# First loads, first sums and the last addition of a two-branch linear-attention kernel in another order

## The chip, the cores and the metric

The kernel runs on one core of a Trainium2 chip. The metric is the device time of one execution in microseconds (us), lower is better. The engines of the core are TensorE (PE; its weight loads are listed as PEld), VectorE (DVE), ScalarE (ACT), GpSimd (POOL) and SyncE (SP). SP computes nothing here: it issues most of the transfers (DMA). ACT issues some as well.

## The reference

```python
def _A_ref(x, wqkv, wo):                       # _B_ref is the same
    B, S, D = x.shape                          # 1, 2048, 640
    H = 32; Dh = D // H
    qkv = (x @ wqkv).reshape(B, S, 3, H, Dh).transpose(2, 0, 3, 1, 4)
    q, k, v = qkv[0], qkv[1], qkv[2]
    phi = lambda t: jnp.where(t > 0, t + 1, jnp.exp(t)) + 1e-6
    pq, pk = phi(q), phi(k)
    kv = jnp.einsum("bhsd,bhse->bhde", pk, v)
    z = jnp.einsum("bhsd->bhd", pk)
    num = jnp.einsum("bhqd,bhde->bhqe", pq, kv)
    den = jnp.einsum("bhqd,bhd->bhq", pq, z)[..., None] + 1e-6
    return (num / den).transpose(0, 2, 1, 3).reshape(B, S, D) @ wo

x = A_x
g = sigmoid((x * gate_w).sum(-1, keepdims=True))
return g * _A_ref(x, A_wqkv, A_wo) + (1 - g) * _B_ref(x, B_wqkv, B_wo)
```

All inputs and the output are bf16. There are 16 row chunks of 128 rows (P = 128), and 640 columns are 5 column chunks (DT = 5) or two halves of HF = 320.

## The kernel before

The kernel works in stages that follow each other on PE. For branch A it makes the k projection with `phi` for all row chunks, mixed with the first half of the q projection; then the rest of q; then the products of x with `phi(k)` (tiles g and gs), from which kv follows; then the same for branch B; then the output, in eight pairs of row chunks, from seven products each (p1 to p7, a Strassen scheme).

*The first stage.* x has to be turned, since PE contracts over partitions: the tile xT holds x transposed, in 5 column chunks. Rows 0 to 255 (chunks 0 and 1) are loaded plain into xn (`load_x`, L116) and turned on PE with an identity matrix (`x_transpose`, L200) into a PSUM tile xt, from which DVE copies to xT (L203). All other rows are turned by the transfer itself (`x_turned`, L119). The k weights wkA are loaded by column chunks (`load_wk`, L122), the q weights wqA in three pieces. A column beside wkA holds `gate_w`, so that the gate's logits come out of the second half of the k sums as a 321st column: gate_w is loaded as five rows (L125), turned on PE (L162), copied by DVE (L164) and written into wkA by POOL (L166).

Before the first data PE runs seven matmuls on constants (L160, tile warm). Then `k_first` makes the k sums of chunks 0 to 3. `k_mm` (L221) is one matmul: a row chunk i, a column chunk c, and a half hf of the columns, into a PSUM tile kA of two banks. Chunks 0 and 1 go together through c = 0 to 2, then each through c = 3 and 4; then chunks 2 and 3 one after the other. `k_done` hands a sum to `phi`: an exponential on ACT (L208), a minimum and an addition on DVE (L213), the maximum with 1 + src on DVE (L217); ACT also copies the logit (L227).

PSUM is handed out in four slots (`ps`), each a tile of two banks; the next user of a slot waits for the last reader of the one before. The first q block (L278), which follows `k_first`, takes slot 2; the next takes slot 3, then come q_single (L288) in slot 0 and chunk 4 in slot 1.

*Order.* The order on each engine in `k_first` and in the output stage is the order in the code (`tc.manual_schedule()`). Eight semaphores serve the transfers in turn, so from the ninth transfer on an issue can wait for the landing of the one eight before it, and holds up its queue meanwhile.

*The end.* A pair's methods are: p7 makes a product on top of the one of p6 in bank x and DVE adds it into one row half (`out_add`, L575); p2 with c11, p4 and p3 make the others. `u25` adds the copy u6 of p6's product and p15 into v, on DVE. Only p3 reads v. The last pair stores its halves separately (L589), two on ACT's queue and two on SP's, and p3 in two parts of 160 columns.

Of the kernel before, what the change touches and what calls it, by code (L numbers as in the profile page):

```python
# [8 lines left out]
P = 128  # L9
FP32 = mybir.dt.float32  # L10
BF16 = mybir.dt.bfloat16
# [3 lines left out]
S, D, H = 2048, 640, 32  # L15
Dh = D // H
DT = D // P
ST = S // P
NB = 4
CB = 4  # L20
HB = 512
HF = D // 2
# [9 lines left out]
def kernel(  # L32
# [11 lines left out]
    nc = tc.nc  # L44
# [13 lines left out]
    def ps_raw(name, slot=None):  # L58

        if slot is None:  # L60
            slot = turn[0]
            turn[0] = (slot + 1) % 4
        return psum.tile([P, 4 * HB], BF16, tag=f"ps{slot}", name=name)

    def ps(name, slot=None):

        return ps_raw(name, slot).bitcast(FP32).rearrange("p (b n) -> p b n", b=2)
# [43 lines left out]
    wk = [None, None]  # L111
# [3 lines left out]
    def load_x(eng, i):  # L115
        eng.dma_start(out=xn[:, i, :], in_=x2[i * P:(i + 1) * P, :])  # L116

    def x_turned(lo, hi):
        nc.sync.dma_start_transpose(out=xT[:, :, lo:hi], in_=x2[lo:hi, :])  # L119

    def load_wk(eng, lo, hi):
        eng.dma_start(out=wk[0][:, lo:hi, 0:D], in_=wq_dram[0][:, lo:hi, D:2 * D])  # L122

    grow = R[0][0:DT, 0:P]
    nc.scalar.dma_start(out=grow, in_=gate_w.rearrange("(c p) -> c p", p=P))  # L125
    load_x(nc.sync, 0)
    load_x(nc.scalar, 1)
    for c, eng in enumerate((nc.sync, nc.scalar, nc.sync, nc.scalar, nc.sync)):
        load_wk(eng, c, c + 1)
    x_turned(2 * P, HB)  # L130
    wq[0] = wpool.tile([P, DT, D], BF16, tag="wq", name="wqA")
    for lo, hi in ((0, 2), (2, 4), (4, DT)):
        nc.sync.dma_start(out=wq[0][:, lo:hi, :], in_=wq_dram[0][:, lo:hi, 0:D])
    for n in range(1, NB):
        x_turned(n * HB, (n + 1) * HB)


    make_identity(nc, ident[:])
# [17 lines left out]
    raw = ps_raw("warm", 3)  # L156
    warm = raw.bitcast(FP32).rearrange("p (b n) -> p b n", b=2)
    one_l, one_r = [nc.const_aps.tensor(1.0, [P, n], BF16) for n in (P, HB)]
    for k in range(7):
        nc.tensor.matmul(warm[:, 0, :], lhsT=one_l, rhs=one_r, start=True, stop=True)  # L160
    gcol = raw[:, 2 * HB:2 * HB + DT]
    nc.tensor.transpose(out=gcol, in_=grow, identity=ident[0:DT, 0:DT])  # L162
    gsb = work.tile([P, DT], BF16, tag="rT", name="gsb")
    nc.vector.tensor_copy(out=gsb[:], in_=gcol)  # L164
    for c in range(DT):
        nc.gpsimd.tensor_copy(out=wk[0][:, c, D:D + 1], in_=gsb[:, c:c + 1])  # L166

    def by_group(dst, lhsT, src, h):

# [28 lines left out]
    def x_transpose(i, pt, cuts=(0, DT)):  # L198
        for c in range(DT):
            nc.tensor.transpose(out=pt[:, c * P:(c + 1) * P], in_=xn[:, i, c * P:(c + 1) * P], identity=ident[:])  # L200
        src = pt[:, 0:D].rearrange("p (c n) -> p c n", c=DT)
        for lo, hi in zip(cuts, cuts[1:]):
            nc.vector.tensor_copy(out=xT[:, lo:hi, i * P:(i + 1) * P], in_=src[:, lo:hi])  # L203
# [15 lines left out]
    def k_mm(b, i, c, pt, hf):  # L219
        w = HF + (hf if b == 0 else 0)  # L220
        nc.tensor.matmul(  # L221
            pt[:, hf, 0:w], lhsT=xT[:, c, i * P:(i + 1) * P], rhs=wk[b][:, c, hf * HF:hf * HF + w],
            start=(c == 0), stop=(c == DT - 1),
        )
# [11 lines left out]

    def k_first():

        pts = [ps("kA", 2 + i) for i in range(2)]
        raw = [ps_raw("xt", i) for i in range(2)]  # L240
        for i in range(2):
            x_transpose(i, raw[i], (0, 2, DT))

        def part(i, cs):
            for c in cs:
                for hf in range(2):
                    k_mm(0, i, c, pts[i], hf)

        for c in range(3):
            for i in range(2):  # L250
                part(i, (c,))
        for i in range(2):
            part(i, (3, 4))
            k_done(0, i, pts[i])
        for i in range(2, CB):
            k_chunk(0, i, i - 2)

    def mixed(t, m):

# [415 lines left out]


    with tc.manual_schedule():
        k_first()
    turn[0] = 2
    for n in range(2):  # L680
# [4 lines left out]
        q_single(0, DT - 1, n)  # L685
    for i in range(hc, ST - 2):
        k_chunk(0, i)
    for n in range(NB):
        lo, hi = max(n * CB, 2), (n + 1) * CB
        nc.sync.dma_start(  # L690
            out=xn[:, lo:hi, :], in_=x2[lo * P:hi * P, :].rearrange("(q p) d -> p q d", p=P)
        )
# [10 lines left out]
    with tc.manual_schedule():  # L703
        k_chunk(0, ST - 2)
        k_chunk(0, ST - 1)
        gate_move()
        k_sum(0, 1)
        q_pass(0, [(m, 1) for m in range(DT)], {0: 2, 1: 3, 2: 4}, (1, 2, 3, 4))
        g_all(0)

        turn[0] = 1
        for i in range(ST):
            k_chunk(1, i)
            if i > 3 and i % 2 == 0:
                m_a(i // 2 - 2)
            if i == 1:
                kv_a()
                wv[1] = load_w(1, "v", nc.sync)
        turn[0] = 2
        TK[1][4] = wpool.tile([P, hc, HF], BF16, tag="wk", name="T4")[:]  # L720
        t = wpool.tile([P, 2, hc, HF], BF16, tag="wo", name="T13")
        TK[1][1], TK[1][3] = t[:, 0], t[:, 1]
        k_sum(1, 1)
        q_pass(1, [(m, h) for h in range(2) for m in range(DT)], {0: 2, 2: 3, 4: 4}, (3, 5, 7))
        g_all(1)
        banks.close()
        outer = ctx.enter_context(late_pool("outer"))
        TM[3] = wpool.tile([P, DT, HF], BF16, tag="wk", name="TM3")
        t = wpool.tile([P, 2, DT, HF], BF16, tag="wq", name="TM12")
        TM[1], TM[2] = t[:, 0], t[:, 1]  # L730
        half = ST // 2
        acc = {k: [bank(outer, f"o{k}{n}") for n in range(2)] for k in "zx"}
        pairs = [Pair(i) for i in range(half)]
        with late_pool("mid") as mid:
            def single(k):
                return bank(mid, f"s{k}")

            first = [single(k) for k in range(4)]

            def m_b(k):  # L740
                part = pk[:, k, :].rearrange("p (b n) -> p b n", b=2)
                w = m_rows(k)[1]
                dst = [first[n] if k == 0 else single(k % 2 * 2 + n) for n in range(2)]
                for n in range(2):
                    m_mm(1, k, dst[n], n)
                for n, copy in enumerate((nc.scalar.copy, nc.vector.tensor_copy if k else nc.scalar.copy)):
                    copy(out=part[:w, n], in_=dst[n][:w, 0:HF])
                m_store(1, k, part)

            kv_mm(1, first[2], 0)  # L750
            kv_mask(first[2], 0)
            pairs[0].p1()
            scale(1, 4, 5, 1)
            kv_mm(1, first[3], 1)
            kv_mask(first[3], 1)
            m_sum(0)
            m_b(0)
            pairs[1].p1()
            m_b(1)
            m_b(2)  # L760
            pairs[2].p1()
            p_sums(part[0], (1,))
            m_b(3)
            m_b(4)
            pairs[3].p1()
            m_b(5)
            for h in range(2):
                m_load(1, h * P // 2, (h + 1) * P // 2)
            pairs[0].p5()
            p_sums(part[1], (1,))  # L770
        pairs[1].p5()
        for n in (2, 3):
            p_sums(part[n], (1,))
        for i in (4, 6):
            for k in range(2):
                pairs[i + k].p1()
                if i == 4:
                    pairs[2 + k].p5()
        for i in range(4, half):
            pairs[i].p5()  # L780
        for n in range(3):
            p_sums(part[n], (2, 4))
        inner = ctx.enter_context(late_pool("inner"))
        acc |= {k: [bank(inner, f"o{k}{n}") for n in range(2)] for k in "wy"}
        for i, b in enumerate("wwy"):
            pairs[i].p2(b)
        for k in (1, 2, 3):
            m_sum(k)
        for i in range(3):
            pairs[i].c11()  # L790
        pairs[0].p6()
        pairs[3].p2("y")
        pairs[0].u25()
        pairs[3].c11()
        ahead = {1: 4, 3: 5, 5: 6}
        later = {1: 2, 3: 4}
        for i in range(half - 1):
            p, after = pairs[i:i + 2]
            p.p7()
            if i in ahead:  # L800
                pairs[ahead[i]].p2()
                pairs[ahead[i]].c11()
            p.p3()
            after.p6()
            after.u25()
            p.p4()
            if i in later:
                p_sums(part[3], (later[i],))
        after.p7()
        after.p2()  # L810
        after.c11()
        after.p4()
        after.p3()
# [30 lines left out]
```

## Time and profile before

| | us |
|---|---|
| median of 3 runs | 187.87 (185.11 to 188.03) |
| the profiled execution | 186.17 |
| its span | 184.4 |
| PE busy in the span | 179.6 |
| DVE busy | 149.6 |
| ACT busy | 75.1 |

The profile is of one execution. Its span runs from the first to the last instruction of the program, and the profiled execution's own time has 1.77 us more around it. Lines of the chain of waits read: start, length, what the time went to. Lines of the timeline read: start, length, engine, source line, operation, tiles as out<-in, count, and in brackets the idle time before it with what ended it. A merged line covers several instructions of one kind. Lines of the answer by stretches read: the stretch, its length, busy time (and count) of PE, PEld, DVE, ACT and POOL, PE's clock, the share of the DMA engines, and GB/s.

### The profile page before, as it was taken

The numbers are of one execution on the slowest core, as the hardware profiler recorded it, in microseconds if no ns is written. First come the engines' busy times: TensorE is split into PE (matmuls) and PEld (weight loads), VectorE is DVE, ScalarE is ACT, GpSimd is POOL, SyncE is SP. The second block draws the span as 40 slices with busy tenths as digits, with TensorE's granted clock in tenths as the row PEclk, the third lists the DMA queues.
The fourth block names the chain that finished last, engine by engine and source line by source line (L and its number), as shares of the span: only waits on it lengthen the run. The fifth ranks groups of instructions, "written<-read, shape, count | busy, mean of one in ns | idle before, by whom it ended". The sixth has DMA issues, their size and how long they took to land.

```text
span 184.4 us, 3339 instructions
## 1 busy us (share of the span) xinstructions
PE 179.6 (97%) x1317; PEld 120.9 (66%) x1317; DVE 149.6 (81%) x239; ACT 75.1 (41%) x128; POOL 3.3 (2%) x22
## 2 busy tenths in 40 slices
PE   8799999999999999999999999999999999999993
PEld 3465756765567777877775555576778777777772
DVE  0276868889999999778788899778799999877863
ACT  2055546547963101357574577631101863111010
POOL 6000000000000000000000000000000000000000
PEclk9999999999999999999999999999999999999999
DMA  5999999024100260151115100000245470133333
GB/s 154 231 279 191 296 375 242 17 37 144 57 0 4 85 235 4 36 174 38 56 33 160 44 2 0 0 0 14 83 127 104 138 215 8 37 107 107 110 108 107
DMA packets 22582, 19.17 MB, mean 104 GB/s; under 512 B 10278, under 2 KB 21798, under 8 KB 22566
## 3 DMA queue, kind: packets, MB, share of 16 engines
q1 hardware_dynamic: 20628, 16.82, 33.5%
q10 hardware_dynamic: 1938, 2.13, 3.5%
q8 instruction: 10, 0.16, 0.4%
q14 instruction: 6, 0.05, 0.1%
HBM read 12.13 MB, written 4.53 MB: 90 GB/s over the span
## 4 chain that ended last, share of the span: by engine, by line
PE 94%; DMA 3%; ACTq 1%; DVE 0%; issue 0%
PE gs L347 17%; PE ox L570 12%; PE kB L221 12%; PE qB L268 12%; PE kA L221 12%; PE qA L268 6%; PE oz L570 6%; PE qA L278 5%; DMA wkA<-in_A_wqkv_dram 3%; PE gB L319 2%; PE gA L319 2%; PE ow L570 2%; PE qA L288 1%; PE s L474 1%; PE mA L474 1%; PE kvA L444 1%
## 5 line engine op out<-in xcount | busy, mean ns | idle before, releaser
L221 PEld LDWEIGHTS <-xT 128*128 128x128 bf16 x320 | 31.1, 98 | 14.0 <-issue 1.3
L213 DVE TENSOR_SCALAR e<-e 128x640 bf16<-128x640 bf16 (+2 forms) x53 | 18.9, 357 | 11.3 <-ACT e L208 10.1
L221 PE MATMUL kA<-wkA,xT 128*128 128x320 bf16 (+1 forms) x160 | 22.6, 300 | 1.2 <-DMA wkA<-in_A_wqkv_dram 1.1
L221 PE MATMUL kB<-wkB,xT 128*128 128x320 bf16 x160 | 23.0, 299 | 0.0
L268 PE MATMUL qB<-xT,wqB 128*128 128x512 bf16 x100 | 21.8, 379 | 0.0
L208 ACT ACTIVATE e<-kB 128x640 bf16<-128x640 f32 x16 | 11.3, 703 | 18.8 <-PE kB L221 18.8
L268 PEld LDWEIGHTS <-wqB 128*128 128x128 bf16 x100 | 11.7, 117 | 9.8 <-issue 0.2
L208 ACT ACTIVATE e<-kA 128x640 bf16<-128x640 f32 x16 | 11.2, 705 | 13.5 <-PE kA L221 13.5
L217 DVE SCALAR_TENSOR_TENSOR pk<-kA,e 128x640 bf16<-128x640 f32 x16 | 13.2, 824 | 2.1
L217 DVE SCALAR_TENSOR_TENSOR pk<-kB,e 128x640 bf16<-128x640 f32 x16 | 13.2, 824 | 1.7
L208 ACT ACTIVATE e<-qB 128x1024 bf16<-128x1024 f32 x10 | 10.2, 1023 | 8.7 <-PE qB L268 7.2
L208 ACT ACTIVATE e<-qA 128x1024 bf16<-128x1024 f32 (+1 forms) x11 | 10.4, 946 | 8.1 <-PE qA L278 5.1
L347 PEld LDWEIGHTS <-xn 128*128 128x128 bf16 x96 | 9.2, 98 | 3.9 <-issue 0.4
L347 PEld LDWEIGHTS <-S 128*128 128x128 bf16 x96 | 9.4, 98 | 3.6
L620 ACT COPY u<-ox 128x320 f32<-128x320 f32 x8 | 3.4, 425 | 20.4 <-PE ox L570 20.4
L268 PE MATMUL qA<-xT,wqA 128*128 128x512 bf16 x50 | 11.0, 379 | 0.0
L570 PEld LDWEIGHTS <-xT 128*128 128x128 bf16 x85 | 8.1, 98 | 2.9
L570 PEld LDWEIGHTS <-pqTB 128*128 128x128 bf16 x80 | 7.8, 98 | 3.2
L570 PEld LDWEIGHTS <-pqTA 128*128 128x128 bf16 x80 | 7.8, 98 | 3.0
L217 DVE SCALAR_TENSOR_TENSOR pqTB<-qB,e 128x1024 bf16<-128x1024 f32 x7 | 8.6, 1224 | 1.1 <-PE qB L268 0.5
L347 PE MATMUL gs<-pk,xn 128*128 128x320 bf16 x64 | 9.4, 299 | 0.0
L268 PEld LDWEIGHTS <-wqA 128*128 128x128 bf16 x50 | 5.9, 117 | 4.8
(126 smaller groups left out, 277.7 us busy)
## 6 DMA issues: line engine op xcount, KB each, us to landing
out_dram<-pk SPq DMA_DIRECT2D x14, 160.0 KB, 1.9
xn<-in_A_x_dram SPq DMA_DIRECT2D x3, 640.0 KB, 7.6
wqB<-in_B_wqkv_dram ACTq DMA_DIRECT2D x1, 800.0 KB, 4.9
wvB<-in_B_wqkv_dram SPq DMA_DIRECT2D x1, 800.0 KB
MA<-mA_dram SPq DMA_DIRECT2D x1, 800.0 KB, 4.2
MB<-mB_dram SPq DMA_DIRECT2D x2, 400.0 KB, 4.4
wqA<-in_A_wqkv_dram SPq DMA_DIRECT2D x2, 320.0 KB, 5.6
woA<-in_A_wo_dram SPq DMA_DIRECT2D x2, 300.0 KB, 10.2
```

The lines of the kernel that those rows point to most:

```text
L208: nc.scalar.activation(out=e[:], in_=src, func=ACT.Exp)
L213: nc.vector.tensor_scalar(e[:], e[:], 1.0, EPS, op0=ALU.min, op1=ALU.add)
L217: nc.vector.scalar_tensor_tensor(out=dst, in0=src, scalar=1.0 + EPS, in1=e[:], op0=ALU.add, op1=ALU.max)
L221: nc.tensor.matmul(pt[:, hf, 0:w], lhsT=xT[:, c, i * P:(i + 1) * P], rhs=wk[b][:, c, hf * HF:hf * HF + w], start=(c == 0), stop=(c == DT - 1),
L268: nc.tensor.matmul(pt[:, u, :], lhsT=mixed(wq[b][:, c, :], m), rhs=xT[:, c, n * HB:(n + 1) * HB], start=(c == 0), stop=(c == DT - 1),)
L278: nc.tensor.matmul(pt[:, u, :], lhsT=mixed(wq[b][:, c, :], m + u), rhs=xT[:, c, n * HB:(n + 1) * HB], start=(c == 0), stop=(c == DT - 1),)
L288: nc.tensor.matmul(pt[:, 0, :], lhsT=mixed(wq[b][:, c, :], m), rhs=xT[:, c, n * HB:(n + 1) * HB], start=(c == 0), stop=(c == DT - 1),)
L319: nc.tensor.matmul(pt[:, hf, 0:HF], lhsT=xn[:, i, c * P:(c + 1) * P], rhs=pk[:, i, hf * HF:(hf + 1) * HF], start=(i == 0), stop=(i == ST - 1),
L347: nc.tensor.matmul(pt[:, n, 0:HF], lhsT=left[:, i, n * P:(n + 1) * P], rhs=right[:, i, :], start=(first and i == 0), stop=(i == hc - 1), s ...
L474: nc.tensor.matmul(dst[:w, 0:HF], lhsT=KVA[:w, k, 0:w], rhs=wo_sb[b][:w, k, n * HF:(n + 1) * HF], start=True, stop=True,)
L570: nc.tensor.matmul(dst, lhsT=left[:, c, r0:r0 + P], rhs=right[:, c, :], start=(first and c == 0), stop=(c == DT - 1), skip_group_check=not ...
L620: nc.scalar.copy(out=self.u6[:], in_=self.at("x"))
```

## The change

Three things change at the start. First, chunks 2 and 3 are no longer turned by a transfer: their rows are loaded plain like those of chunks 0 and 1 and turned on PE. Second, wkA comes by column halves: the left halves of column chunks 0-1 and 2-4 first, then the two further row chunks of x, then the right halves in three pieces, and all of wkA on SP's queue. `k_first` makes the left sums of all four chunks first (the gate's column belongs to the right half), then the right halves, each followed by its `phi`. Third, the warm-ups are six matmuls of 512 columns and three of 128, and the gate's column is turned after the transposes of chunks 0 and 1 instead of ahead of them; ACT copies it instead of DVE. The transposed xt tiles and the kA tiles take other slots.

At the end, the last pair's `u25` comes after its p7 instead of ahead of the pair before's p4.

```diff
+    def load_wk(lo, hi, hf):
+        d0 = hf * HF
+        nc.sync.dma_start(out=wk[0][:, lo:hi, d0:d0 + HF], in_=wq_dram[0][:, lo:hi, D + d0:D + d0 + HF])
...
-    nc.scalar.dma_start(out=grow, in_=gate_w.rearrange("(c p) -> c p", p=P))
-    load_x(nc.sync, 0)
-    load_x(nc.scalar, 1)
-    for c, eng in enumerate((nc.sync, nc.scalar, nc.sync, nc.scalar, nc.sync)):
-        load_wk(eng, c, c + 1)
-    x_turned(2 * P, HB)
...
+    def first_loads():
+        load_x(nc.sync, 0)
+        load_x(nc.scalar, 1)
+        nc.scalar.dma_start(out=grow, in_=gate_w.rearrange("(c p) -> c p", p=P))
+        for lo, hi in ((0, 2), (2, DT)):
+            load_wk(lo, hi, 0)
+        load_x(nc.sync, 2)
+        load_x(nc.sync, 3)
+        for lo, hi in ((0, 2), (2, 4), (4, DT)):
+            load_wk(lo, hi, 1)
+        for lo, hi in ((0, 2), (2, 4), (4, DT)):
+            nc.sync.dma_start(out=wq[0][:, lo:hi, :], in_=wq_dram[0][:, lo:hi, 0:D])
+        for n in range(1, NB):
+            x_turned(n * HB, (n + 1) * HB)
...
-    for k in range(7):
-        nc.tensor.matmul(warm[:, 0, :], lhsT=one_l, rhs=one_r, start=True, stop=True)
...
+    def warm_up(n, w):
+        for k in range(n):
+            nc.tensor.matmul(warm[:, 0, 0:w], lhsT=one_l, rhs=one_r[:, 0:w], start=True, stop=True)
+    def gate_column():
...
-    nc.vector.tensor_copy(out=gsb[:], in_=gcol)
+        nc.scalar.copy(out=gsb[:], in_=gcol)
...
     def k_first():
-        pts = [ps("kA", 2 + i) for i in range(2)]
-        raw = [ps_raw("xt", i) for i in range(2)]
-        for i in range(2):
-            x_transpose(i, raw[i], (0, 2, DT))
-        def part(i, cs):
-            for c in cs:
-                for hf in range(2):
-                    k_mm(0, i, c, pts[i], hf)
-        for c in range(3):
-            for i in range(2):
-                part(i, (c,))
-        for i in range(2):
-            part(i, (3, 4))
-            k_done(0, i, pts[i])
-        for i in range(2, CB):
-            k_chunk(0, i, i - 2)
+        pts = {}
+        def part(i, hf, cs=range(DT)):
+            for c in cs:
+                k_mm(0, i, c, pts[i], hf)
+        warm_up(6, HB)
+        warm_up(3, P)
+        xt = [ps_raw("xt", 1), ps_raw("xt", 0)]
+        for i in range(2):
+            x_transpose(i, xt[i], (0, 2, DT))
+        gate_column()
+        for i in range(2):
+            pts[i] = ps("kA", 2 + i)
+            part(i, 0, (0, 1))
+        part(0, 0, (2, 3, 4))
+        x_transpose(2, ps_raw("xt", 1))
+        part(1, 0, (2, 3, 4))
+        x_transpose(3, ps_raw("xt", 0))
+        for i in (2, 3):
+            pts[i] = ps("kA", 3 - i)
+            part(i, 0)
+        for i in range(CB):
+            part(i, 1)
+            k_done(0, i, pts[i])
...
-    for n in range(NB):
-        lo, hi = max(n * CB, 2), (n + 1) * CB
+    for n in range(1, NB):
+        lo, hi = n * CB, (n + 1) * CB
         nc.sync.dma_start(
             out=xn[:, lo:hi, :], in_=x2[lo * P:hi * P, :].rearrange("(q p) d -> p q d", p=P)
...
             after.p6()
-            after.u25()
+            if not after.last:
+                after.u25()
             p.p4()
...
         after.p7()
+        after.u25()
         after.p2()
```

## The prediction, made before the changed kernel had run

> **What bounds the kernel now.** I read the page first (busy shares, the slices, the chain of shares by line), then the chain of waits for the first 14 us, then TensorE's (PE's) timeline for the first 8 us, then busy times by stretch, then VectorE's (DVE's) timeline at the end. From the page:
>
> ```profile
> PE 179.6 (97%) x1317; PEld 120.9 (66%) x1317; DVE 149.6 (81%) x239; ACT 75.1 (41%) x128; POOL 3.3 (2%) x22
> ...
> PE   8799999999999999999999999999999999999993
> ...
> DMA  5999999024100260151115100000245470133333
> ...
> L221 PE MATMUL kA<-wkA,xT 128*128 128x320 bf16 (+1 forms) x160 | 22.6, 300 | 1.2 <-DMA wkA<-in_A_wqkv_dram 1.1
> ```
>
> PE is busy for 97% of the span; only the first two slices (4.6 us each) and the last are not full. The one wait of note in all 160 kA matmuls is 1.1 us on a piece of wkA. The chain that ended last, cut to the start, says where:
>
> ```profile
> 1.81 5.19 DMA wkA<-in_A_wqkv_dram
> 7.00 0.04 issue
> 7.04 5.07 PE kA L221 x36
> ```
>
> From 7.04 on it is PE alone, through all later stages up to 180.94. So what this change moves at the start reaches the end in full: the number to forecast is the moment when the first qA matmul (L278) starts, 11.95 us now. PE before that:
>
> ```profile
> 0.84 3.14 PE L160 MATMUL warm<-const-bfloat16-1.0 128*128 128x512 bf16 x7 [0.84 <-PEq L828]
> 3.92 0.18 PE L162 MATMUL warm<-ident,R 5*128 5x5 bf16 x1
> 4.03 0.94 PE L200 MATMUL xt<-ident,xn 128*128 128x128 bf16 x10
> 5.05 0.91 PE L221 MATMUL kA<-wkA,xT 128*128 128x320 bf16 x4
> 7.04 1.25 PE L221 MATMUL kA<-wkA,xT 128*128 128x320 bf16 x8 [1.09 <-DMA wkA<-in_A_wqkv_dram]
> ```
>
> Read the counts: seven warm-ups of 512 columns start 0.427 us apart ((3.14-0.58)/6), while qA's 20 of the same width later take 4.48 us, 0.216 each. So the first 4 us run at half rate, although the granted-clock row shows 9 in every slice; in the middle of the ten transposes the spacing drops from 0.107 to 0.056 us, at about 4.45. After that a kA matmul costs 0.1355 us (20 in 2.72 in the chain). Only four kA matmuls run between 5.05 and 7.04.
>
> ```profile
> 2.50:3.50 1.00, 1.00 (x4) 0.29 (x2) 0.00 (x0) 0.72 (x1) 0.87 (x4) 1.00 1.04 291
> 3.50:4.50 1.00, 1.00 (x8) 0.55 (x6) 0.17 (x1) 0.56 (x1) 0.14 (x2) 1.00 0.81 247
> 4.50:5.50 1.00, 0.92 (x10) 0.39 (x7) 0.80 (x4) 0.00 (x0) 0.52 (x5) 1.00 1.04 359
> 5.50:6.00 0.50, 0.45 (x2) 0.21 (x3) 0.22 (x1) 0.00 (x0) 0.00 (x0) 1.00 1.29 308
> 6.00:7.00 1.00, 0.00 (x0) 0.00 (x0) 0.00 (x0) 0.00 (x0) 0.00 (x0) 1.00 1.86 85
> ```
>
> The last number is GB/s. It runs at 250 to 360 and falls to 85 in 6.0 to 7.0, exactly where PE waits and where the first transposing load (L119, issued at 2.67) is in the queues. Summed with 134 for 1.5 to 2.5, 425 KB have moved by 3.5, 672 by 4.5, 1,031 by 5.5 and 1,185 by 6.0.
>
> **The change, part by part.**
>
> *Loads.* The transposing load of chunks 2 and 3 goes; two plain loads of 164 KB replace it, and the later 320 KB load of the same rows (L690) goes too. SP issues xn0, wkA left c0-1, left c2-4, xn2, xn3, right c0-1, right c2-3, right c4, then wqA in three and the three transposing loads. An issue costs 0.39 to 0.58 us (rows of L116, L133), so right c4 is out by about 4.8 us and wqA by about 6.4, before the queues reach them. From the seventh on SP waits for a piece eight issues earlier (xn1, xn0, the gate row and so on); these land first, so I put the waits at nothing. If xn1 came late, only right c2-3 and what follows would, which have 0.9 us in hand (below). The gate row moves behind xn1 on ScalarE's (ACT's) queue: 1.41 instead of 0.80, needed at 4.7; xn1 comes 0.6 earlier. The table load (1.28 us, at 2.77) has no issue of wkA before it any more.
>
> Arrival, by the running sum above plus 0.5 us from the last byte to landing (my estimate; a whole 80 KB store at the end lands 1.6 us after issue) and 0.15 for rows of 640 bytes instead of 1,280: left c0-1 closes 492 KB, lands 4.4; left c2-4 737 KB, 5.3; xn2 901 KB, 5.8; xn3 1,065 KB, 6.3; then at 330 GB/s (the answer for 9.5 to 11.5) right c4 7.5 and wqA 9.9. Loads in 640-byte rows are not in this trace; the 640-byte stores at the end reach 349 GB/s, so the bounds are 0 and, at the 247 of 3.5 to 4.5, 0.6 us more.
>
> *PE.* Six long warm-ups and three of a quarter: 0.84 + 6 x 0.427 + 3 x 0.107 = 3.72. I keep the pause of 0.14 (3.78 to 3.92) that the first wait behind them had: 3.86. Transposes to first kA matmul took 5.05 - 4.03 = 1.02: 4.88. The second chunk's first matmul came 0.46 behind that: 5.34, where the new wait for the ACT copy of the gate column (0.17 on DVE, done by about 5.1) is over. Then, at 0.1355 each: two left matmuls of chunk 1 and three of chunk 0 to 6.02 (c2-4 landed at 5.3), five transposes 0.28 (xn2 at 5.8), three matmuls to 6.71, five transposes to 6.99 (xn3 at 6.3), left of chunks 2 and 3, with their 640-column copies (0.29 for 256 columns, 0.35 for 384, so about 0.47) just covered by the work between, to about 8.4. Right halves of four chunks: 4 x 0.68 to 11.12. The gate columns that POOL writes (0.66 us, over by about 6) are then long there.
>
> *A wait that takes over.* The first q block writes the bank of chunk 0. Now chunk 0 ends early and its ACT and DVE work hides behind chunks 1 to 3; afterwards it ends 2.04 us before q. Its exponential starts 0.2 after its last matmul (8.88) and DVE lets go at 10.09 + 0.82 = 10.91: 2.03 later. So q can't start before 9.08 + 0.2 + 2.03 + 0.05 = 11.36: 0.24 of PE idle. DVE then works four chunks at 1.19 us until 14.9 instead of 14.5; its idle 0.88 before the first q row (15.36) takes that up.
>
> So q starts at 11.36 instead of 11.95: -0.59.
>
> *The clock.* One execution shows full rate from 4.45, 3.6 us after the first warm-up. Before, PE had little to do between there and 7.04; afterwards each us at half rate from 4.88 on is 0.5 us lost. Were the turn at 4.3, the gain would be 0.05; one more such stretch later, at 8.05, the loss is (8.05-4.88)/2 = 1.6. I take +0.3, near the end that was seen. The Trainium skill (TensorE: Matmul & The Clock Gate, Part 1) says that full clock follows a busy window of about 3.4 us whose phase the kernel doesn't control; the turn after 3.6 us agrees. By that rule, with every phase as likely, this term would be some 0.8 us, an estimate, and the sum 186.4.
>
> *The tail.* The last pair's v (L575, 0.49) moves behind the sum of p7.
>
> ```profile
> 178.64 0.49 DVE L575 TENSOR_TENSOR v<-u,xn 128x320 f32<-128x320 f32 x1 [0.65 <-ACT u L620]
> 179.05 0.98 DVE L575 TENSOR_TENSOR pk<-ox,xn 128x320 bf16<-128x320 f32 x2
> 180.22 0.49 DVE L575 TENSOR_TENSOR pk<-ow,xn 128x320 bf16<-128x320 f32 x1 [0.19 <-PE ow L570]
> 180.97 0.49 DVE L575 TENSOR_TENSOR pk<-ox,xn 128x320 bf16<-128x320 f32 x1 [0.25 <-PE ox L570]
> ```
>
> The second of the pair at 179.05 is p7's sum; it starts at 179.55, and p7's last matmul ends at 179.51 (178.67 + 0.84). So it is bound by PE, and gains 0.01 at most. v then runs at 179.96, the next sum slips from 180.22 to 180.37, and the one after still starts by PE at 180.97 (180.37 + 0.41 is earlier). The last two parts are unmoved: 0, bounds -0.05 and +0.15 (should that slip reach the end).
>
> **Sum.** The profiled execution took 186.17 (span 184.4, 1.77 around it): 186.17 - 0.59 + 0.3 + 0 = 185.9 us. It was itself 1.7 us below the median 187.87 of runs from 185.11 to 188.03; against that median 185.9 is -1.1%.
>
> **The rivals.**
>
> *Pieces still late.* Left c2-4 has 0.3 us in hand, xn2 0.2. A piece that lands as late as wkA's second did (7.00, with 1,185 KB moved by 6.0) holds PE at 5.4 to 6.6 and q starts at about 12.5: 186.17 + 0.6 + 0.3 = 187.1. For it: that piece took 5.2 us from issue. Against: the transposing load beside which it starved is gone from there.
>
> *Clock late: the slower side.* Full rate came after 3.6 us of nearly unbroken work. PE now has a wait at 5.1 to 5.3, and 20 transposes among the first matmuls instead of ten. If the count isn't full by then and starts again at 5.34, the turn is at 8.94: 1.8 us lost in that stretch and 0.35 in the first transposes and matmuls, q at 13.5, +1.6, 187.8. If transposes break it each time, it starts again with the right halves: the left part from 5.34 takes 6.1 instead of 3.1, then 3.6 at half rate, q at 16.0, +4.0, 190.2. I take 188.5, nearer the first, since here the turn came among ten transposes. It decides from the point where idle ahead of 4.45 grows past the 0.14 seen here. Against: up to 4.9 PE has as little idle as before. The Trainium skill (TensorE: Matmul & The Clock Gate, Part 4) says that transposes don't count as work for the clock, which speaks for this case; the trace doesn't decide it.
>
> *More gain.* Pieces as forecast, the turn at 4.3, no pause after the warm-ups: q at 11.2, 185.3; with the 1.06 by which the lowest run lies under the profiled one, 184.3. For it: the spread of the runs before may lie in just the wait that goes. Against: the bank of chunk 0 stops q from starting earlier.
>
> **How the numbers follow.** Forecast 0.55 (185.2 to 186.6), late pieces 0.17 (187.1), late clock 0.14 (188.5), more gain 0.14 (184.3). The range, 184.3 to 188.6, leaves out the lower half of the last case and the part of the late clock beyond 188.6, some 0.13 together. Against the median of 187.87, 2% (about what a measurement of this kernel can tell from no change) is 3.8 us: faster takes less than 184.1, 0.1, from the lower part of the last case; slower takes over 191.6, 0.06, a late clock together with late pieces; within 2%, 0.84.
>
> **What would show it.** Right: first kA matmul at 4.9, no wait on wkA over 0.3 us, kA matmuls without gaps from 5.3, a PE wait of about 0.2 at the first qA, which starts near 11.4; GB/s over 250 through 6 to 9 us; in the tail p7's sum one 0.04 after its last matmul and the last stores where they were, counted from the last matmul. Wrong: a wait of a microsecond on wkA or xn, kA matmuls 0.27 apart behind 5 us, or q starting after 11.95.

## The result, and the profile after

The changed kernel takes 186.19 us in the median (185.81 to 186.50, 22 runs), the kernel before 186.04 (184.94 to 189.77, 22 runs beside it). The ratio is 1.0031, 95% interval 1.0017 to 1.0045: slower by 0.3%, far inside 2%. The forecast was 185.9, down from a median that three runs had put at 187.87. The size is close (0.3 us), which is luck, as the part on the prediction shows; the sign is wrong. The changed kernel's lowest time is 0.87 above the lowest of the kernel before, its highest 3.27 below the highest. The ratio compares only runs that lie within 1.5% of the fastest of their kernel, so four of before's runs (187.87 to 189.77) are not in it.

The profiled execution took 186.44, with a span of 184.7. Its page:

```profile
PE 180.3 (98%) x1329; PEld 121.7 (66%) x1329; DVE 150.1 (81%) x240; ACT 75.2 (41%) x129; POOL 3.3 (2%) x22
...
L234 PE MATMUL kA<-wkA,xT 128*128 128x320 bf16 (+1 forms) x160 | 23.0, 300 | 0.7 <-DMA wkA<-in_A_wqkv_dram 0.7
```

The wait for wkA has gone from 1.1 us to 0.7, but PE's busy time has gone from 179.6 to 180.3: ten more transposes, and warm-ups of about the same length (3.04 us instead of 3.14). The chain of waits begins with a late piece again, now the left half of c2-4, and then runs over the bank of chunk 0 (lines: start, length, what):

```profile
1.73 4.65 DMA wkA<-in_A_wqkv_dram
...
6.42 0.57 PE kA L234 x3
...
7.99 2.14 PE kA L234 x15
...
10.15 0.71 ACT e L221
...
11.36 0.84 DVE pk L230
...
12.24 1.89 PE qA L298 x8
```

PE's timeline of the same stretch:

```profile
4.80 0.91 PE L234 MATMUL kA<-wkA,xT 128*128 128x320 bf16 x4
6.42 0.57 PE L234 MATMUL kA<-wkA,xT 128*128 128x320 bf16 x3 [0.71 <-DMA wkA<-in_A_wqkv_dram]
...
7.89 4.28 PE L234 MATMUL kA<-wkA,xT 128*128 128x320 bf16 x30
12.24 2.10 PE L298 MATMUL qA<-xT,wqA 128*128 128x512 bf16 x9
```

The first kA matmul starts at 4.80 (forecast 4.88). PE has four matmuls to do, as before, and is through with them at 5.53 (the last two start at 5.26, and each takes 0.1355); the next starts at 6.42. The listed 0.71 is counted from the end of the fourth's result; 0.89 is what is lost. The first qA matmul starts at 12.24, against 11.95 in the profile before. From there nothing differs: 0.29 at q is 0.29 in the span (184.43 to 184.72 unrounded) and 0.27 in the time. The profiled execution (186.44) is among the slowest of its 22.

By stretches (the columns as before, GB/s last):

```profile
2.50:3.50 1.00, 1.00 (x5) 0.44 (x4) 0.00 (x0) 0.64 (x1) 0.86 (x4) 1.00 1.00 327
3.50:4.50 1.00, 1.00 (x13) 1.00 (x12) 0.05 (x1) 0.00 (x0) 0.00 (x0) 1.00 0.97 282
4.50:5.50 1.00, 0.98 (x10) 0.47 (x8) 0.97 (x4) 0.17 (x1) 0.40 (x4) 1.00 0.80 246
5.50:6.00 0.50, 0.21 (x2) 0.01 (x1) 0.00 (x0) 0.00 (x0) 0.26 (x3) 1.00 1.03 283
6.00:7.00 1.00, 0.58 (x6) 0.35 (x6) 0.00 (x0) 0.00 (x0) 0.00 (x0) 1.00 1.01 326
```

The bytes came as forecast: with 152 KB ahead of 2.5, 761 KB had moved by 4.5, and left c2-4 closes 737. The rate while PE waits is 283 to 326 (5.5 to 7.0), nowhere near the 85 of before. Yet the piece had landed in full only at 6.37. The trace shows what held it: of the 16 shares of that piece (one for each DMA engine) 13 were in by 5.18, the last two at 6.28 and 6.37. A piece has landed when its slowest share is in, and a sum of bytes over all engines doesn't show that one lags. Single packets were slow at that time: of those that started between 4.36 and 4.86, two of 640 bytes took 460 and 558 ns and one of 1,280 bytes 425, where packets of these sizes mostly take 32 and 55. The records don't name a packet's engine, so that these packets are the late shares' own is likely but not shown, and what made them slow stays open.

In the tail (DVE's timeline) the v of the last pair runs where the forecast put it:

```profile
179.84 0.49 DVE L595 TENSOR_TENSOR pk<-ox,xn 128x320 bf16<-128x320 f32 x1 [0.19 <-PE ox L590]
180.25 0.48 DVE L595 TENSOR_TENSOR v<-u,xn 128x320 f32<-128x320 f32 x1
180.65 0.48 DVE L595 TENSOR_TENSOR pk<-ow,xn 128x320 bf16<-128x320 f32 x1
181.26 0.49 DVE L595 TENSOR_TENSOR pk<-ox,xn 128x320 bf16<-128x320 f32 x1
```

p7's sum (179.55 before) and the one of 181.26 (180.97 before) stand 0.29 later, the shift of q and no more. The sum between has slipped from 180.22 to 180.65: the shift and about the 0.15 that were forecast, and it ends before 181.26.

### The profile page after: what moved, and what is told of

It reads as the page before. It is cut to its first block, busy times and chain, and to the rows that moved or that the text cites. A ratio compares the mean times of both kernels' runs of the same rounds, so it can differ in the third digit from the quotient of the medians.

```text
span 184.7 us, 3366 instructions
## 1 busy us (share of the span) xinstructions
PE 180.3 (98%) x1329; PEld 121.7 (66%) x1329; DVE 150.1 (81%) x240; ACT 75.2 (41%) x129; POOL 3.3 (2%) x22
## 4 chain that ended last, share of the span: by engine, by line
PE 93%; DMA 3%; DVE 1%; SPq 0%; issue 0%; ACT 0%; DVEq 0%
PE gs L367 17%; PE ox L590 12%; PE kB L234 12%; PE qB L288 12%; PE kA L234 11%; PE qA L288 6%; PE oz L590 6%; PE qA L298 5%; DMA wkA<-in_A_wqkv_dram 3%; PE gB L339 2%; PE gA L339 2%; PE ow L590 2%; PE qA L308 1%; PE s L494 1%; PE mA L494 1%; PE kvA L464 1%
## 5 line engine op out<-in xcount | busy, mean ns | idle before, releaser
L288 PEld LDWEIGHTS <-wqB 128*128 128x128 bf16 x100 | 11.7, 117 | 9.8 <-issue 0.2
L288 PE MATMUL qA<-xT,wqA 128*128 128x512 bf16 x50 | 11.0, 379 | 0.0
L298 PE MATMUL qA<-xT,wqA 128*128 128x512 bf16 x40 | 9.0, 379 | 0.1
```

Of the source, the lines that this page charges most:

```text
L288: nc.tensor.matmul(pt[:, u, :], lhsT=mixed(wq[b][:, c, :], m), rhs=xT[:, c, n * HB:(n + 1) * HB], start=(c == 0), stop=(c == DT - 1),)
L298: nc.tensor.matmul(pt[:, u, :], lhsT=mixed(wq[b][:, c, :], m + u), rhs=xT[:, c, n * HB:(n + 1) * HB], start=(c == 0), stop=(c == DT - 1),)
```

## The experiments

The first theory (A) was that left c2-4 alone held PE up: without it q starts about 0.9 us earlier. The rival (B) was that all early pieces land a microsecond later than I had put them, so that the next one takes its place. The landings in the changed kernel's profile speak for it: xn2 landed at 6.80, xn3 at 7.25, right c0-1 at 7.68, right c4 at 8.31, for forecasts of 5.8, 6.3 and, for the last, 7.5. A third question came up on the way: what the kernel before has really to lose in this stage.

All times in us. "turn" is where the clock records show TensorE going to full rate, or, with "about", where the spacing of matmuls halves. The ratio is to runs of the kernel before on the same chip, with its 95% interval. The rows come from several chips, and the median of before differed there: 186.04 beside the changed kernel; 185.49 (35 runs) beside left_from_c01, left_and_rows_from_first, right_of_chunk0_early and before_new_tail; 185.22 (15 runs) beside rows_before_second_left and whole_chunks_plain_rows; 185.27 (35 runs) beside the other four. So rows are compared by their ratios; their medians can differ by some tenths without a cause in the kernel.

| run | median (lowest to highest), runs | ratio | profile: q start | its time | turn |
|---|---|---|---|---|---|
| before, first profile | | | 11.95 | 186.17 | 4.45 |
| after | 186.19 (185.81 to 186.50), 22 | 1.0031 | 12.24 | 186.44 | 4.37 |
| left_from_c01 | 186.17 (185.72 to 186.59), 12 | 1.0032 [1.0013, 1.0051] | 12.12 | 186.32 | 4.95 |
| left_and_rows_from_first | 185.74 (185.31 to 186.44), 12 | 1.0014 [0.9994, 1.0034] | 11.93 | 186.16 | about 6.0 |
| right_of_chunk0_early | 186.01 (185.59 to 186.20), 12 | 1.0017 [1.0000, 1.0035] | 11.39 | 185.59 | 3.79 |
| no_late_data_no_bank_wait | 185.69 (185.30 to 186.54), 12 | 1.0018 [0.9990, 1.0045] | 11.90 | 186.12 | 6.64 |
| rows_before_second_left | 186.15 (185.98 to 186.53), 11 | 1.0036 [1.0010, 1.0062] | 12.04 | 186.23 | about 5.7 |
| second_left_on_act | 186.33 (186.10 to 186.97), 12 | 1.0036 [1.0004, 1.0067] | 11.66 | 186.19 | 4.56 |
| whole_chunks_plain_rows | 188.24 (187.86 to 188.37), 5 | 1.0145 [1.0100, 1.0190] | 13.77 | 188.29 | 6.58 |
| whole_chunks_plain_rows_2 | 186.47 (186.14 to 186.77), 12 | 1.0048 [1.0024, 1.0073] | 12.08 | 186.63 | about 6.5 |
| before_again_1 | one run | | 11.32 | 185.51 | 6.40 |
| before_again_2 | one run | | 10.84 | 185.04 | 3.71 |
| before_new_tail | 186.19 (185.02 to 188.17), 12 | 1.0018 [0.9990, 1.0046] | 13.60 | 187.81 | 3.47, and again 10.30 |
| before_rows1_on_sp | 185.70 (185.05 to 187.83), 12 | 1.0010 [0.9974, 1.0046] | 10.81 | 185.05 | about 5 |

Read two columns together first: the profiled time less the start of q is 174.19 to 174.24 in eleven of the fourteen rows, whatever the first stage looked like. The three others (second_left_on_act and both with whole chunks) have 174.52 to 174.55. So the start of q is what the change and the edits of the first stage decide, and the tail adds nothing. It also lets a time without a profile be read: the changed kernel's median of 186.19 has q at about 11.99, its lowest at 11.61, and the profiled execution's 12.24 is a late one.

One more row of numbers belongs to all that follows. Five profiles have the changed kernel's loads in its order. In them left c2-4 landed at 6.37 (after), 6.25 (left_from_c01), 5.48 (left_and_rows_from_first), 5.77 (right_of_chunk0_early) and 6.09 (no_late_data_no_bank_wait). It was later than the forecast 5.3 each time, but by 0.2 to 1.1 us.

**left_from_c01.** The left sums read column chunks 0 and 1 of wkA only, so they don't wait for left c2-4 (these sums are then of other columns).

```diff
...
-                k_mm(0, i, c, pts[i], hf)
+                k_mm(0, i, c, pts[i], hf, c if hf else c % 2)
```

The new last argument of `k_mm` is the column chunk of wkA.

> The changed kernel, but the left k sums of the first four row chunks multiply the weights of column chunks 0 and 1 also in the place of 2 to 4 (this part of the result is changed), so that the matmuls no longer wait for the second wkA piece; all loads stay. Theory A, one late piece: PE's 0.87 us of idle goes, the first qA matmul moves from 12.24 to about 11.4, median about 185.3. Theory B, the last shares of every piece are about a microsecond late: the wait moves to the third row chunk of x, which landed at 6.80, its transposes start at 6.85 as now, the first qA matmul stays within 0.1 of 12.2, median 186.1 to 186.2.

PE's timeline:

```profile
5.00 1.19 PE L235 MATMUL kA<-wkA,xT 128*128 128x320 bf16 x7
6.73 0.45 PE L213 MATMUL xt<-ident,xn 128*128 128x128 bf16 x5 [0.54 <-DMA xn<-in_A_x_dram]
```

Seven matmuls run through without the piece, and then PE waits for xn2, which landed at 6.68. q is at 12.12 and the median where it was, as B said. The pieces behind are late as well; A falls.

**left_and_rows_from_first.** In addition the transposes of chunks 2 and 3 read the rows of chunks 0 and 1, so nothing loaded behind left c0-1 is waited for ahead of the right halves.

```diff
...
-        x_transpose(2, ps_raw("xt", 1))
+        x_transpose(2, ps_raw("xt", 1), src_i=0)
...
-        x_transpose(3, ps_raw("xt", 0))
+        x_transpose(3, ps_raw("xt", 0), src_i=1)
```

> As left_from_c01, and row chunks 2 and 3 are turned from the rows of chunks 0 and 1 (their k sums are changed too), so that neither wkA's second piece nor the two later row chunks of x are waited for; all loads stay. Theory A: no further gain over left_from_c01, about 185.3. Theory B: only here the lateness goes, until the right halves (landed 7.68, 8.10, 8.31) are wanted at about 8.4; first qA matmul at 11.3 to 11.5, 0.8 to 0.9 earlier than the changed kernel, 185.3. A third view, that some other wait would take over (the bank of chunk 0, DVE): less than 0.4 gained, 185.8 or more.

B's 185.3 is reached by the lowest run alone (185.31, 0.50 under the changed kernel's lowest). The median is 0.45 lower, by the two ratios 0.3, and their intervals overlap: so in a usual run the late pieces cost at most some 0.3 us, and not the 0.9 of the profile. The profiled execution itself shows q at 11.93: with no wait on data there, the late turn (about 6.0) costs instead.

**right_of_chunk0_early.** The right half and `phi` of chunk 0 come ahead of the left half of chunk 3, so that chunk 0's bank is free earlier.

```diff
-        for i in (2, 3):
-            pts[i] = ps("kA", 3 - i)
-            part(i, 0)
-        for i in range(CB):
+        pts[2] = ps("kA", 1)
+        part(2, 0)
+        part(0, 1)
+        k_done(0, 0, pts[0])
+        pts[3] = ps("kA", 0)
+        part(3, 0)
+        for i in range(1, CB):
```

> The changed kernel with the right half of chunk 0 (and its phi) ahead of the left half of chunk 3. The bank that the first q block waits for comes free 0.68 earlier. If the 0.24 us of idle ahead of the first qA matmul is the bank's wait: idle gone, qA at 12.0, 185.95. If it were a transfer (wqA) the start would stay at 12.24 and the time at 186.2. If the right half's first piece came later than 8.6 in most runs, it would be slower than 186.2.

PE's timeline:

```profile
5.81 0.57 PE L234 MATMUL kA<-wkA,xT 128*128 128x320 bf16 x3 [0.28 <-DMA wkA<-in_A_wqkv_dram]
...
11.39 1.89 PE L301 MATMUL qA<-xT,wqA 128*128 128x512 bf16 x7
```

q starts at 11.39 and not at the 12.0 expected, since left c2-4 came 0.6 earlier in this execution. The bank's part can be read apart from that: from the first matmul behind the wait on left c2-4 to q it is 5.82 us in the changed kernel (6.42 to 12.24) and 5.58 here (5.81 to 11.39), with the same work at full rate. Those 0.24 are the wait on the bank, of the size forecast. The last kA matmul and q start 0.38 apart there and 0.136 here, the spacing of kA matmuls. The median is 0.18 below the changed kernel's, which the overlapping intervals don't tell from no difference.

**no_late_data_no_bank_wait.** Both edits together.

> left_and_rows_from_first and right_of_chunk0_early together: no wait for the second left piece or the later rows (the k sums of the first four chunks are changed in part), and the bank free earlier. If the waits for pieces and the bank's wait are the whole of what the changed kernel loses beside the ten transposes, first qA matmul at about 11.1 to 11.2 where the clock turns by 4.5, later by up to a microsecond where it turns at 6 or later; 185.1 to 185.9, lowest 185.1. If something else stands in front of qA, the lowest stays at 185.3 (left_and_rows_from_first).

The chain of waits is PE alone:

```profile
5.11 1.82 PE kA L236 x7
...
12.06 1.94 PE qA L303 x9
```

No wait from 5.1 on, and still q starts at 11.90: the turn was at 6.64, and seven kA matmuls took 1.82 us where the changed kernel's rate gives 0.95. Five of the twelve runs lie at 185.30 to 185.39 (185.1 was expected of the lowest), which I take for the order's floor: with every wait away, it only reaches the ordinary runs of the kernel before.

**rows_before_second_left.** The rows of chunks 2 and 3 are loaded ahead of left c2-4, and the sums follow: c0-1 of all four chunks first, and the right half of chunk 0 ahead of the last left work. The edit's part on the loads:

```diff
-        for lo, hi in ((0, 2), (2, DT)):
-            load_wk(lo, hi, 0)
+        load_wk(0, 2, 0)
         load_x(nc.sync, 2)
         load_x(nc.sync, 3)
+        load_wk(2, DT, 0)
...
```

> The changed kernel with the rows of chunks 2 and 3 loaded ahead of the second left piece, the first left piece used for all four chunks, and the right half of chunk 0 ahead of the last left work. If every piece lands in turn about a microsecond late (theory B), the rows land at 6.0 and 6.5 and the left piece at 7.2; first qA matmul at 11.6, 185.6. If the second left piece is late for a reason of its own (its size or rows), it lands past 7.5 and nothing is gained: 186.1.

The rows landed at 5.37 and 6.05, left c2-4 at 7.10: each piece by its place in the line. There is no gain (q at 12.04 for 11.6 expected); the profile has a late turn (about 5.7) and a wait of 0.31 for DVE's copy to xT.

**second_left_on_act.** Left c2-4 goes on ACT's queue behind xn1, the gate row behind it.

```diff
...
+        load_wk(0, 2, 0)
+        load_wk(2, DT, 0, nc.scalar)
         nc.scalar.dma_start(out=grow, in_=gate_w.rearrange("(c p) -> c p", p=P))
-        for lo, hi in ((0, 2), (2, DT)):
-            load_wk(lo, hi, 0)
```

> The changed kernel with the second left piece issued on ACT's queue right behind the second row chunk, the gate row after it. If the piece is late because so much lies ahead of it on one queue, it now lands at about 5.0 and xn2 at about 6.0, first qA matmul at 11.5 to 11.8, 185.6. If single slow packets on one or two engines hold whatever is in flight then, it lands at 5.5 to 6.4 still, xn2 at 6.2 to 6.8: 186.0 to 186.2.

PE's timeline, at the start and in the output stage:

```profile
5.18 0.17 PE L175 MATMUL warm<-ident,R 5*128 5x5 bf16 x1 [0.32 <-DMA R<-in_gate_w_dram]
...
160.33 0.84 PE L590 MATMUL ox<-TM,D 128*128 128x320 bf16 x5 [0.21 <-ACT u L640]
```

Here the piece landed at 5.18, xn2 at 5.67 and xn3 at 6.09, 1.1 to 1.2 us earlier than in the changed kernel's profile; against the earliest of the five profiles above the piece is only 0.3 earlier, so how much of it is the second queue's doing one profile can't tell. The gate row is late instead (0.32). q gains 0.58. But at 160.33 PE waits for ACT's copy u ahead of a p7 product and loses 0.32 us more than the changed kernel loses there; the two kernels with whole chunks have this at the same product. The copy itself starts 1.25 us after the first matmul of the product that it copies, against 0.94 in the changed kernel, so the delay lies ahead of the copy. What brings it about stays open.

**whole_chunks_plain_rows** and **whole_chunks_plain_rows_2.** wkA by whole column chunks on two queues and the sums in the order of before, but chunks 2 and 3 plain and turned on PE: no half pieces, and no transposing load ahead. The gate's column is turned first again. The second has the transposes of chunks 2 and 3 ahead of both `k_done`.

```diff
-        for lo, hi in ((0, 2), (2, DT)):
-            load_wk(lo, hi, 0)
+        for c, eng in enumerate((nc.sync, nc.scalar, nc.sync, nc.scalar, nc.sync)):
+            eng.dma_start(out=wk[0][:, c:c + 1, 0:D], in_=wq_dram[0][:, c:c + 1, D:2 * D])
...
-        for lo, hi in ((0, 2), (2, 4), (4, DT)):
-            load_wk(lo, hi, 1)
...
```

> The changed kernel with one part undone: wkA again as whole column chunks on two queues and the sums in the order of the kernel before, the gate's column turned first; rows of chunks 2 and 3 stay plain loads turned on PE. Theory C, the transposing load made wkA's second piece late in the kernel before: that piece lands at about 5.6, no PE idle over 0.3 us, no wait for a bank; first qA matmul at about 11.1 and 185.2, with few runs over 186. Theory B, slow last shares belong to any load at this time: second piece at 6 to 7, first qA matmul at 11.6 to 12.3, 185.8 to 186.3.

> whole_chunks_plain_rows with the turned rows' copies ahead of the first two phi on DVE, where in that run they stood behind one and held PE for 1.42 us. Its pieces landed at 6.19 (second), 7.01 (fourth) and 7.29, 8.64 (rows). Theory B: PE waits 0.2 to 0.5 in several places, first qA matmul at 11.4 to 11.8, 185.6 to 186.0, no gain over the kernel before beside it. Theory C: 185.2 or less.

The first lost 1.42 us by its own order: DVE's copy of the turned rows stood behind a `phi`, and PE waited for it.

```profile
10.81 3.13 PE L232 MATMUL kA<-wkA,xT 128*128 128x320 bf16 x20 [1.42 <-DVE xT L214]
```

In the second the second to fifth pieces landed at 6.15, 5.96, 6.99 and 6.81, the rows at 7.29 and 9.02. The lateness needs neither half pieces, nor one queue, nor a transposing load beside it. The median of 186.47 is above what either theory gave (C 185.2, B 185.6 to 186.0); the profile has a late turn and the wait for u in it.

**before_again_1** and **before_again_2.** The kernel before, unchanged, profiled again.

> The kernel before, profiled again. Runs of it gather near 185.1, 186.1 and 188. If the time follows from the landing of wkA's second piece, a run near 185.1 has it at 6.0 or earlier and the first qA matmul at 10.8 to 11.0; a run near 188 shows half rate again after 7 us.

> The kernel before, profiled once more, as before_again_1: time minus the profiled 186.17 equals the start of the first qA matmul minus 11.95, within 0.1, whichever it is.

PE's timeline of the second:

```profile
4.88 6.13 PE L221 MATMUL kA<-wkA,xT 128*128 128x320 bf16 x40
10.84 3.40 PE L278 MATMUL qA<-xT,wqA 128*128 128x512 bf16 x15
```

And its chain of waits:

```profile
1.81 4.09 DMA wkA<-in_A_wqkv_dram
...
5.94 5.07 PE kA L221 x36
```

The second piece of wkA landed at 5.92 and 5.90 instead of 7.00. The times lie 0.66 and 1.13 below the first profile's, q 0.63 and 1.11. PE still waits for the piece in before_again_2, but 0.23 us (its fourth kA matmul is through at 5.71) instead of the 1.25 lost in the first profile (5.79 to 7.04, of which the page lists 1.09). In before_again_1 the clock turned late, at 6.40; the first four matmuls run at half rate, and the last of them starts at 6.15, behind the landing of the piece.

So the long wait on wkA is not in every execution. The 22 runs of before beside the changed kernel fall in three groups: nine from 184.94 to 185.29, nine from 185.90 to 186.39, where the first profile (186.17) lies, and four from 187.87 up. By the sum of 174.2 the first group has q at 10.7 to 11.1 and the second at 11.7 to 12.2; whether a late piece is behind each run of the second group is not recorded.

**before_new_tail.** The kernel before with only the last `u25` moved.

```diff
-            after.u25()
+            if not after.last:
+                after.u25()
...
+        after.u25()
```

> The kernel before with only the last pair's u25 moved behind p7. By the step of the prediction: p7's sum is bound by PE, nothing gained or lost, within 0.1 us of the kernel before beside it. If the order of DVE at the end mattered: 0.1 to 0.2 us faster (or slower).

No difference that can be measured (1.0018, interval across 1). Its profiled execution, 187.81 us, is of the sort of the 187 to 190 that before shows now and then. PE's timeline, then the answer by stretches:

```profile
7.18 6.58 PE L221 MATMUL kA<-wkA,xT 128*128 128x320 bf16 x36 [1.26 <-DMA wkA<-in_A_wqkv_dram]
```

```profile
3.50:6.80 3.30, 1.96 (x17) 0.98 (x16) 1.27 (x5) 0.55 (x1) 0.66 (x5) 1.00 1.38 252
6.90:10.20 3.30, 3.02 (x12) 1.73 (x12) 0.00 (x0) 0.00 (x0) 0.00 (x0) 0.50 0.90 251
10.40:11.40 1.00, 1.00 (x9) 0.71 (x8) 0.14 (x1) 0.88 (x3) 0.00 (x0) 1.00 1.16 304
```

The second piece landed at 7.14. In the stretch with the waits PE was busy for 1.96 of 3.30 us at full clock; then the clock stood at 0.50 for 3.41 us, with kA matmuls 0.267 apart, and only then came back. In this execution the late piece cost its wait and, on top, half of a stretch of 3.4 us.

**before_rows1_on_sp.** The kernel before with xn1 on SP's queue, which lets ACT issue wkA's second piece first.

```diff
-    load_x(nc.scalar, 1)
+    load_x(nc.sync, 1)
```

> The kernel before with one edit: the second row chunk of x is issued on SP behind the first, so that wkA's second piece is the first long load on ACT's queue. By the landings of the kernel before (second piece at 5.90 and the second row chunk at 4.5 in its good runs, 7.0 in others), the second piece lands at about 5.0, the row chunk at 3.7; PE then runs without a wait from 5.2 on, first qA matmul at 10.5 to 10.7, 184.7 to 184.9, and runs over 186 become fewer. Rival: the first piece, now third on SP, comes after 4.9 and takes back the gain: 185.1 to 185.3.

The second piece landed at 4.39 and the profile has no wait on wkA, but the first kA matmul starts at 5.36 instead of 4.88 (the turn came at about 5, during the transposes, and PE waits for DVE's copy), and q at 10.81, where before_again_2 has it too, instead of the 10.5 to 10.7 expected. No gain that can be measured (1.0010, interval across 1). Two of its twelve runs are above 187, where fewer over 186 were expected. No version here is measurably faster than the kernel before.

## Why the prediction was wrong

Where the time up to q went, in two profiles with an early turn (from the rows above; kA matmuls at 0.1355, transposes at 0.056):

| us | before_again_2 | after |
|---|---|---|
| first kA matmul | 4.88 | 4.80 |
| 40 kA matmuls | 5.42 | 5.42 |
| transposes of chunks 2 and 3 | | 0.56 |
| wait for a piece of wkA (the second; left c2-4, 5.53 to 6.42) | 0.23 | 0.89 |
| bank of chunk 0 | | 0.24 |
| smaller waits | 0.31 | 0.33 |
| first qA matmul | 10.84 | 12.24 |

- **The step that failed first: the arrival of the pieces.** The running sum of bytes was right. The step from it to a landing, 0.5 us after a piece's last byte, was not: left c2-4 should have landed at 5.3 and took until 6.37; xn2 and xn3 were 1.0 late each, right c4 0.8. The forecast q of 11.36 and some 0.88 of wait on that piece give 12.24, which is what the profile has. This is the rival of late pieces, at a smaller size than I gave it (12.5), and the profile shows a bad case of it: with left c2-4 landing anywhere from 5.48 to 6.37 and the median run's q at 11.99, the usual loss is likely smaller. What I held against the rival, that the transposing load had starved wkA's second piece and was gone, is not borne out: whole_chunks_plain_rows_2 has pieces at 6 to 7 us with no transposing load ahead, and in the first profile of before 15 of 16 shares of the second piece were in by 5.67. The 85 GB/s look like an effect of the late share: of the transposing load's packets (256 bytes, 18 ns mostly), the 20 that stood longest began between 5.91 and 6.51 and all ended at 7.54 to 7.58, half a us after that share's 7.00; in before_again_2, where the last share came at 5.90, such packets ended at 6.57 to 6.60. No edit tried this.
- **The step that gave the wrong sign: the base of the sum.** I took 0.59 off an execution whose long wait on wkA only part of the executions have, and what the change adds (0.56 of transposes, 0.24 of a bank) every execution pays. In before_again_2 q starts at 10.84, earlier even than my 11.36. Had every step of the sum come true, the kernel would have lost 0.5 us against this one. The three runs of before (185.11 to 188.03) had in fact told that its time varies by more than the wait that I took for fixed. That the median of 187.87 would be the kernel's usual time was wrong too: with 22 runs it is 186.04. Of the gain of 1.97 us that the forecast showed against 187.87, the change's own part was 0.29 (0.59 less 0.3); the rest was the distance of the profiled execution from that median.
- **Right: the wait on chunk 0's bank.** Forecast 0.24; seen as 0.24 ahead of q (10.15 to 12.24 in the chain), and gone in right_of_chunk0_early, whose way to q is shorter by just that.
- **Right: the tail at nothing.** Its sums moved with q, and before_new_tail can't be told from before.
- **Close by chance: the clock's +0.3 and with it the total.** In after the turn came at 4.37, in the first profile of before at 4.45, and I took it for something that only the change might move. It moves by itself, from 3.47 to 6.64 in the ten profiles that have a record of it; the sum's +0.3 did not show in after, whose turn came ahead of the first kA matmul. The ten further transposes have no visible part in the turn: they come behind the turn in after, and before_again_1 and _2 are one kernel and have 6.40 and 3.71. The Trainium skill (TensorE: Matmul & The Clock Gate, Part 1) gives a free-running window of 3413 ns and hence a turn that depends on its phase; the spread of 3.17 us and the 3.41 us at half clock in before_new_tail agree with it. The same section of the Trainium skill lets the clock fall back after an idle window; before_new_tail fell back with PE busy for 1.96 of 3.30 us, and the measurement decides. The rival of a clock put late by the change didn't show: no run of the changed kernel is above 186.50. Its dearer case, that transposes don't count as work, is spoken against by whole_chunks_plain_rows: PE was busy there for 2.32 us, all warm-ups, up to 3.17, and the clock stayed; it turned one window of 3.41 us later, in which transposes were 1.25 of 3.18 us of work and the rest 1.93. That 185.9 lies so near is luck: in the profile 0.88 was lost that the sum hadn't, and the 0.3 that it had for the clock stood against it.
- **The narrow spread is the one thing gained.** The changed kernel's 22 runs lie within 0.7 us, those of before within 4.8. That PE waits for data until 6.4 anyway hides a late turn: in no_late_data_no_bank_wait, without that wait, the spread is 1.2 again. That the missing falls back to half clock come from the shorter wait (0.89 lost, instead of 1.25 in the first profile of before and 1.43 in before_new_tail) fits, but was not tried.

## What to carry to other kernels

Profile the kernel before more than once ahead of a sum: a wait of a microsecond on an early load may be there in some executions only, while a change that takes it away is paid for in every one by its own work (here 0.56 us of transposes and 0.24 of a bank). In the first microseconds, date a piece by when its slowest share landed in several traces, not by bytes over rate. Where PE is the bound, work moved onto it has to be paid for by a wait that every execution has.

## What the runs showed of the hardware

- Early pieces land by their slowest DMA engine: of left c2-4, 13 of 16 shares were in by 5.18 and the last at 6.37; single packets of 1,280 bytes, which mostly take 55 ns, took up to 1.23 us (at 7.27) in that trace and up to 1.17 us (at 4.61) in that of before_new_tail. With the same loads in the same order, left c2-4 landed between 5.48 and 6.37 in five executions.
- The granted clock changes as if windows of 3.41 us followed one another: in the ten profiles with a record, the stretches between two changes last 3.413, 177.493 or 180.906 us, which are 1, 52 and 53 times 3.413. By these windows, one needn't be full to bring full rate: the one that ended at 3.47 in before_new_tail did so with PE busy for 2.63 us, the one that ended at 3.22 in no_late_data_no_bank_wait didn't with 2.38.
- The clock can go back to half rate without a full idle window: 1.96 us busy in 3.30, then 3.41 us at half rate. In the first profile of before, with PE busy for 2.24 us in the window that ended at 7.86, it didn't. Where between them the limit lies is open.
- Three kernels (second_left_on_act and both with whole chunks), which differ from the changed kernel only in the first stage, lose 0.32 us more to ACT's copy u 150 us later, at one p7 product, in their profiled executions. Why is open.
